# Clustered attention with a SoLU feed-forward layer on one core: the first batch's later head pairs loaded with both heads of a token side by side and sorted to clusters in one pass, u centred in place of w_out, and a new order by hand

## The chip, the cores and the metric

The kernel runs on one core of one Trainium2 chip. The metric is the device time of one execution in microseconds (us), the median of three runs. Both versions are compared by that number.

## The reference

Attention over B = 4 batches, H = 8 heads, S = 768 tokens, D = 64, in which a query sees only the keys of its own cluster, and then a feed-forward layer over all 3072 tokens. All inputs and the output are float32.

```python
q_n, k_n, c_n = (each row divided by its norm)            # centroids: [8, 16, 64]
q_assign = argmax(einsum('bhsd,hcd->bhsc', q_n, c_n), -1)  # 16 clusters a head
k_assign = argmax(einsum('bhsd,hcd->bhsc', k_n, c_n), -1)
mask = q_assign[:, :, :, None] == k_assign[:, :, None, :]
attn = softmax(where(mask, q @ k.T / sqrt(64), -1e9))
x = (attn @ v) with the heads side by side                 # [3072, 512]

h = x @ w_in                                               # [3072, 1024]
solu = h * softmax(h)
ln = (solu - mean(solu)) / sqrt(var(solu) + 1e-6) * g_ln
out = ln @ w_out                                           # [3072, 512]
```

## The kernel before, in words

**How it is built.** All work is cut into operations, each added with `add(name, engine, cost, key, function, needs, after, ...)` to an object of the class `Weave`. The order in which an engine runs them is written out by hand in five tables, `ORDER["SP"]`, `["POOL"]`, `["PE"]`, `["DVE"]`, `["ACT"]`: a kind of operation and a count, such as `E6` for the next six exponentials. `AWAY` lists the operations that another engine than their default one does. `run` only walks through these queues, so an engine does its operations strictly in the table's order and waits at each for what it needs.

**The attention.** 4 batches of 4 head pairs. For each pair q and k are loaded (`ld`, DMAs issued by SP), turned so that d lies on partitions (`tp` on PE at L396 and L403 with copies `xa`, `xb` out of PSUM at L422 and L430 for batch 0; `xt` on DVE for the others) into a tile xt, and cast to bf16 into qk (`ca`, L468 to L472). A product with the centroids (`cl`, on PE, PSUM tile csc) and four DVE steps (`tb`, `mx`, `oh`, `ot`) give a one-hot row of each token's cluster; 32 such rows are placed below the d rows of qk (`pl` on POOL, DVE or, as a DMA, on SP; `bl` blanks the other head's). With them the scores (`S`, L627, PE, into a ring of three PSUM banks sps or into a spare bank of hreg) come out so large where clusters agree that the exponential (`E`, L635, ACT) gives the mask too. `V` (L654, PE) multiplies e by v, which is loaded by `lv` and cast by `cv` (L558), and `N` (L666, L679, DVE) divides by the sum.

**E sets the shape of the start.** 294 E in all. Batch 0 has 24 of 384 columns for pair 0, whose tokens are done in two halves, and then 54 of 512 columns for pairs 1 to 3. So "the 25th E" is the first of pairs 1 to 3, and it needs pair 1's q and k, turned, cast and sorted to clusters.

**The loads of pairs 1 to 3 of batch 0.** `load_twelve` (L377) issues one DMA of 384 KB for q and one for k: a partition takes twelve tokens in a row, 3072 bytes, of head 0 on partitions 0 to 63 and of head 1 on 64 to 127. Once turned, even and odd tokens lie on the two halves of the partitions, not the two heads. So the copies sort by `by_two`, casts and placements write every other block (`every_other`), and the cluster product takes two accumulating passes (L484) with centroids masked by parity, `c_by_two`, which a second centroid transposition (`cq`, L909) and `cf` (L919) prepare in memory that w_out_c uses later.

**The feed-forward layer.** 24 tiles of 128 tokens, f = 0 to 23, six per batch, woven between the next batch's attention and, at the end, alone. For each: x turned (`tx`, a DMA), h = x @ w_in (`h`, L744, PE, into two of the three banks of hreg), its maximum (`hm`, L750, DVE), e = exp(h - max) with its sum (`ex`, L756, ACT), u = e * h (`u`, L763, DVE; three buffers), variance (`bn`, L774, and `ag`, L778, DVE), u turned into uT (`tu`: a DMA at L768, or for the last tiles `ptu` on PE, L732, with a copy at L738), y = uT @ w_out_c (`y`, L813, PE), a factor alpha per token (`at`, `al` on POOL), the evacuation times alpha (`sc`, L830 ACT or L832 DVE) and the store (`ou`, SP). The mean of solu is taken out beforehand, in the weights: w_out_c is g * w_out less its mean over d_ff. For that DVE sums g * w_out (`su`, L595 and L598, eight steps), PE takes the mean over partitions (`me`, L604, two matmuls) and DVE subtracts (`ce`, L607, eight steps).

**Around the start.** w_in and w_out are loaded by `li` and `lo`, four DMAs each; `wi` (L578, POOL) casts w_in to bf16. Until data comes PE runs idle matmuls (`wm`, 25 of them, and `fl`, two each, L859).

## Time and profile before

| | before |
|---|---|
| three runs, us | 224.49, 224.18, 224.29 |
| median, us | 224.29 |
| profiled execution: span from first to last instruction, us | 222.4 |
| profiled execution: instructions | 6852 |
| mean granted TensorE clock | 0.999 |
| DMA | 38.74 MB in 122,433 packets, 111,448 of them under 512 bytes |
| HBM | 23.11 MB read, 6.29 MB written |

The profile is of one execution, and its times count from the first instruction; the run time of an execution holds what lies around the span too, so the median stands 1.9 us above it. Engines: PE is the matrix engine, PEld its weight loads, DVE, ACT and POOL the vector, scalar and general engines, SP the one that only issues DMAs. A line of a group reads: source line, engine, operation, out<-in, the shapes, the count; then busy us and the mean ns of one; then the idle us just before these instructions and what ended most of it. A line of the timeline reads: start, length, engine, source line, operation, out<-in, count, and in brackets the wait before and who ended it. The windows view gives for each stretch its length, then busy us (and count) of PE, PEld, DVE, ACT and POOL, the granted clock, the share of the 16 DMA engines, and GB/s.

### The profile page before, as it was taken

Reading aid. Unit: us, or ns where it says so; the run is one execution under the profiler, and the core shown is the slowest. Engines: PE = TensorE matmul, PEld = TensorE weight load, DVE = VectorE, ACT = ScalarE, POOL = GpSimd, SP = SyncE. Lnnn points to the kernel's source line nnn. Section 1 sums busy time; section 2 is a strip of 40 time slices with the busy share of each in tenths; the row PEclk is TensorE's granted clock in tenths of the full one; section 3 lists DMA queues with packets and bytes.
Section 4 is the critical chain, followed back from the end, with each engine's and each line's share of the span. In section 5 each row is a group of like instructions: output and inputs, shape, how many; then the busy total and the mean of one; then the engine's idle time right before and its main releaser. Section 6 shows DMA issues by size and latency. Waiting matters only on the chain.

```text
span 222.4 us, 6852 instructions
## 1 busy us (share of the span) xinstructions
PE 214.8 (97%) x2518; PEld 151.8 (68%) x2548; DVE 199.1 (90%) x363; ACT 194.7 (88%) x382; POOL 126.6 (57%) x252
## 2 busy tenths in 40 slices
PE   8999899999999999999999999999999999999993
PEld 7765577767777687777777666676767767665452
DVE  2789999999999999899989999999999979999891
ACT  3899999999999999999999989999999989795352
POOL 3189597759884986188837674783746101226131
PEclk9999999999999999999999999999999999999999
DMA  6998989797799979899999897998922928565623
GB/s 157 352 388 221 193 165 284 203 172 165 127 175 237 180 141 215 136 193 166 153 211 239 156 185 150 151 168 158 230 99 50 115 78 145 117 165 121 166 98 143
DMA packets 122433, 38.74 MB, mean 174 GB/s; under 512 B 111448, under 2 KB 117152, under 8 KB 122400
## 3 DMA queue, kind: packets, MB, share of 16 engines
q1 hardware_dynamic: 121680, 37.82, 79.8%
q10 hardware_dynamic: 720, 0.49, 0.7%
q8 instruction: 20, 0.33, 0.7%
q14 instruction: 13, 0.11, 0.1%
HBM read 23.11 MB, written 6.29 MB: 132 GB/s over the span
## 4 chain that ended last, share of the span: by engine, by line
PE 91%; DVE 3%; issue 2%; ACT 2%; DVEq 0%; ACTq 0%
PE sps L627 27%; PE hreg L744 18%; PE yps L813 17%; PE ops L654 16%; PE csc L489 4%; PE hreg L627 2%; PE idle_p L859 2%; PE csc L484 1%; PE hreg L403 1%; PE hreg L396 1%; ACT qk L468 1%; PE hreg L813 1%; ACT e L635 1%; DVE u L763 1%; DVE w_sum L598 1%
## 5 line engine op out<-in xcount | busy, mean ns | idle before, releaser
L635 ACT ACTIVATE e<-sps 128x512 bf16<-128x512 f32 (+1 forms) x276 | 143.2, 609 | 10.2 <-PE sps L627 9.8
L627 PE MATMUL sps<-qk 96*128 96x256 bf16 (+5 forms) x600 | 87.4, 263 | 0.7 <-ACT e L635 0.4
L627 PEld LDWEIGHTS <-qk 96*128 96x128 bf16 (+1 forms) x636 | 59.6, 121 | 24.5 <-issue 8.8
L654 PEld LDWEIGHTS <-e 128*128 128x128 bf16 x1152 | 49.9, 97 | 9.3 <-issue 1.9
L654 PE MATMUL ops<-v,e 128*128 128x65 bf16 x1152 | 54.3, 193 | 0.4 <-DVE x L679 0.4
L744 PE MATMUL hreg<-w_in_sb,xT 128*128 128x512 bf16 x177 | 48.3, 378 | 0.8
L813 PE MATMUL yps<-w_out_c,uT 128*128 128x512 bf16 x169 | 45.1, 379 | 0.8
L540 POOL COPY qk<-oht 32x384 f32<-32x384 f32 (+1 forms) x49 | 24.2, 494 | 21.5 <-DVE oht L521 15.7
L763 DVE TENSOR_TENSOR u<-e_sb,hreg 128x1024 bf16<-128x1024 bf16 (+1 forms) x25 | 29.1, 1169 | 2.7 <-ACT e_sb L756 2.1
L774 DVE BATCH_NORM_STATS2 bs<-u 128x6 f32<-128x512 bf16 x48 | 31.3, 677 | 0.0
L750 DVE TENSOR_REDUCE nmax<-hreg 128x1 f32<-128x1024 f32 x24 | 29.1, 1213 | 2.0 <-PE hreg L744 1.7
L756 ACT ACTIVATE e_sb<-hreg,nmax 128x1024 bf16<-128x1024 f32 x24 | 26.9, 1121 | 4.5 <-DVE nmax L750 4.4
L790 POOL TENSOR_SCALAR esq<-es,mv 128x1 f32<-128x1 f32 x24 | 8.3, 344 | 33.6 <-DVE mv L778 30.3
L813 PEld LDWEIGHTS <-uT 128*128 128x128 bf16 x200 | 18.0, 97 | 13.1 <-issue 0.3
L744 PEld LDWEIGHTS <-xT 128*128 128x128 bf16 x192 | 17.6, 97 | 11.3 <-ACT e L635 0.3
L472 POOL TENSOR_SCALAR qk<-xt 64x768 bf16<-64x768 f32 (+1 forms) x27 | 22.2, 823 | 3.5 <-DVE xt L444 1.7
L444 DVE STREAM_TRANSPOSE xt<-raw 128x768 f32<-128x768 f32 x24 | 22.2, 949 | 0.0
L470 POOL CAST qk<-xt 64x768 bf16<-64x768 f32 (+1 forms) x25 | 20.9, 836 | 1.2
L679 DVE TENSOR_TENSOR x<-ops,den 128x256 bf16<-128x256 f32 (+1 forms) x39 | 18.9, 486 | 1.3
L784 POOL TENSOR_SCALAR es<-esum 128x1 f32<-128x1 f32 x24 | 5.6, 236 | 20.9 <-ACT e_sb L756 20.4
L793 POOL TENSOR_TENSOR alpha<-esq,halves 128x1 f32<-128x1 f32 x24 | 13.8, 574 | 2.0
L830 ACT ACTIVATE y<-yps,alpha 128x512 f32<-128x512 f32 x15 | 10.4, 695 | 4.3 <-PE yps L813 3.0
(85 smaller groups left out, 206.9 us busy)
## 6 DMA issues: line engine op xcount, KB each, us to landing
vf<-in_v_dram SPq DMA_DIRECT2D x16, 384.0 KB, 4.6
out_dram<-y SPq DMA_DIRECT2D x23, 256.0 KB, 2.5
raw<-in_q_dram SPq DMA_DIRECT2D x50, 96.0 KB, 3.8
raw<-in_k_dram SPq DMA_DIRECT2D x50, 96.0 KB, 3.0
w_g<-in_moe_w_out_dram SPq DMA_DIRECT2D x4, 512.0 KB, 8.3
w_st<-in_moe_w_in_dram SPq DMA_DIRECT2D x4, 512.0 KB, 6.2
raw<-in_q_dram SPq DMA_DIRECT2D x3, 384.0 KB, 6.0
raw<-in_k_dram SPq DMA_DIRECT2D x3, 384.0 KB, 7.8
```

Of the source, the lines that this page charges most:

```text
L444: nc.vector.transpose(xt[:], raws[b, p, i][:].rearrange("p j c -> p (j c)"))
L472: VEC[e].tensor_scalar(dst, src, scalar1=inv_C, scalar2=1.0, op0=Alu.mult, op1=Alu.mult)
L540: ins = VEC[e].tensor_copy(dst.bitcast(F32), src.bitcast(F32).unsqueeze(1) .to_broadcast([NB, 2, n // 2]))
L627: ins = nc.tensor.matmul(sps_[n, k][:, c0:c0 + w], side(b, h // 2, 1, h % 2, keys)[r], side(b, h // 2, 0, h % 2, slice(s0 * P, s0 * P + w) ...
L635: ins = nc.scalar.activation(es[n, k][:, :w], sps_[n, k][:, :w], Act.Exp, scale=exp_scale, bias=-exp_scale)
L654: nc.tensor.matmul(opss[g][:, s, :VW], es[n, k][:, c0:c0 + P], v1[slot(b, h // 2)][:, h % 2, kt, :VW], start=(kt == 0), stop=(kt == n_t - 1))
L744: uses(nc.tensor.matmul(hreg[:, at(f, f2)[1], :], xTs[f][:, dc, :], w_in_sb[:, dc, f2 * FF2:(f2 + 1) * FF2], start=(dc == 0), stop=(dc == ...
L750: uses(nc.vector.tensor_reduce(ff[f, "nmax"][:], pair_of(f), axis=AXY, op=Alu.max, negate=True), *both(f))
L756: uses(nc.scalar.activation(ff[f, "e"][:], pair_of(f), Act.Exp, bias=ff[f, "nmax"][:], accum_out=ff[f, "esum"][:]), *both(f))
L763: uses(nc.vector.tensor_tensor(ff[f, "u"][:, r], ff[f, "e"][:, r], pair_of(f)[:, r], op=Alu.mult), *both(f)[r])
L774: nc.vector.bn_stats(ff[f, "bs"][:, f2, :], ff[f, "u"][:, f2, :])
L813: ins = nc.tensor.matmul(dst, ff[f, "uT"][:, at(f, f2)[0] * (n_fc // 2) + c, :], w_out_c[:, fc, cols], start=(fc == fcs[0] and turn == 0 i ...
```

## The change

Four things are done together.

1. **Loads of pairs 1 to 3 of batch 0.** `load_pair` issues two DMAs of 192 KB for q and two for k, one a head. A partition takes six tokens in a row of a head, and the two heads of a token stand side by side in the tile: 768 pieces of 256 bytes a DMA. Turned, the two heads lie on the two halves of the partitions. `load_twelve`, `by_two`, `every_other`, `own_two`, `c_by_two`, `cq` and `cf` go; copies, casts and placements use the plain forms of the other batches, and the cluster product is one pass with `c_bd`.
2. **Centring.** w_out is only scaled by g (`scale_w_out`, `gw`, eight steps: five on POOL and three on DVE); `su`, `me` and `ce` go. u is made by an operation that also sums it over its row (su, over d_ff), and a new step `cu` replaces u in place by d_ff * u - su before the variance and the transposition: tiles 0, 1, 2, 5, 6, 10, 12, 14, 16, 19, 20, 22 on DVE, tile 23 in two halves on DVE, the other 11 on POOL. The small number in the root is scaled by d_ff.
3. **The first scores** have to come after all idle matmuls (`wm`, `fl`).
4. **New tables** `ORDER` and `AWAY`. Among much else, the copies and casts that ACT did among pair 0's E go to DVE and POOL or ahead of the first E, all four transpositions of pair 1 stand ahead of the first scores, the loads of w_out go behind those of w_in, ten instead of five placements are DMAs by SP, DVE has five fewer evacuations `sc`, and tile 22's copies of uT go from DVE to ACT.

The core of the diff, without what only falls away and without the costs in `add`, which now have no effect on the order:

```diff
...
     ORDER["PE"] = """
-        fl wm tp2 cp fl4 cl tp2 fl4 cl fl tp S2 cq S tp S tp S2 tp S tp2 S2 cl S V3 S2 tp3 S gt V3
+        fl7 wm tp2 cp tp fl cl fl tp fl tp2 cl tp2 S3 cl S3 tp2 S2 tp S tp S gt V3 S2 cl S V3 S2 tp
...
     ORDER["ACT"] = """
-        wa xa2 ca2 xa2 xb ca4 E6 xa E2 xa E xa ca E3 xa3 E4 ca E2 xa E53 ex E13 ex E5 sc E3 ex E11
+        wa xa xb xa ca2 xa ca xb xa2 ca xa E9 xa E64 ex E8 ex E12 ex sc E13 ex E4 sc E3 ex E3 sc E16
...
-    def load_twelve(b, p, i):
-        raws[b, p, i] = ld.tile([P, n_j, NB], F32, name="raw")
-        nc.sync.dma_start(out=raws[b, p, i][:].rearrange("p j c -> p (j c)"),
-                          in_=SRC[i][b, 2 * p:2 * p + 2].rearrange("h (q t) d -> (h q) (t d)",
-                                                                   q=D))
+    def by_turn(b, p, i):
+        return raws[b, p, i][:].rearrange("p j c -> p (j c)").rearrange("p (t m) -> p t m", m=P)
+
+    def load_pair(b, p, i, hh):
+        if (b, p, i) not in raws:
+            raws[b, p, i] = ld.tile([P, n_j, NB], F32, name="raw")
+        nc.sync.dma_start(out=by_turn(b, p, i)[:, :, hh * D:(hh + 1) * D],
+                          in_=SRC[i][b, 2 * p + hh].rearrange("(p t) d -> p t d", p=P))
...
-        if twelve(b, p):
-            dst = by_two(b, p, i).rearrange("p h t (q u) -> p h t u q", u=2)[:, :, :, hf, :]
-            src = src.rearrange("p (t h q) -> p h t q", h=2, q=D)
...
-        if twelve(b, p):
-            for c in range(4):
-                i, part = divmod(c, 2)
-                nc.tensor.matmul(csc[c * NB:(c + 1) * NB, :], c_by_two[:, p, 2 * part + hh, :],
-                                 by_two(b, p, i)[:, hh].rearrange("p t n -> p (t n)"),
-                                 start=(hh == 0), stop=(hh == 1), tile_position=(0, c * NB))
-        for c in range(4) if not twelve(b, p) else ():
+        for c in range(4):
...
-    def mean_w_out(x):
-        cols = slice(x * FF2 // 2, (x + 1) * FF2 // 2)
-        uses(nc.tensor.matmul(hreg[:, 2, cols], g_mean[:], w_sum[:, cols]), 2)
-
-    def centre_w_out(fc):
-        uses(nc.vector.scalar_tensor_tensor(out=w_out_c[:, fc, :], in0=w_g[:, fc, :],
-                                            scalar=g_ln2[:, fc:fc + 1], in1=hreg[:, 2, :],
-                                            op0=Alu.mult, op1=Alu.subtract), 2)
+    def scale_w_out(fc, e):
+        VEC[e].tensor_scalar(w_out_c[:, fc, :], w_g[:, fc, :], scalar1=g_ln2[:, fc:fc + 1],
+                             scalar2=None, op0=Alu.mult)
...
-        uses(nc.vector.tensor_tensor(ff[f, "u"][:, r], ff[f, "e"][:, r], pair_of(f)[:, r],
-                                     op=Alu.mult), *both(f)[r])
+        was = ff[f, "su"][:] if half else 0.0
+        ff[f, "su"] = sm.tile([P, 1], F32, name="su", bufs=6)
+        uses(nc.vector.tensor_tensor_reduce(
+            out=ff[f, "u"][:, r], in0=ff[f, "e"][:, r], in1=pair_of(f)[:, r], scale=1.0, scalar=was,
+            op0=Alu.mult, op1=Alu.add, accum_out=ff[f, "su"][:]), *both(f)[r])
+
+    def f_centre(f, e, half=None):
+
+        u = ff[f, "u"][:] if half is None else ff[f, "u"][:, half]
+        VEC[e].tensor_scalar(u, u, scalar1=float(d_ff), scalar2=ff[f, "su"][:], op0=Alu.mult,
+                             op1=Alu.subtract)
...
-        nc.gpsimd.tensor_scalar(ff[f, "es1"][:], ff[f, "esum"][:], scalar1=1e-3, scalar2=None,
+        nc.gpsimd.tensor_scalar(ff[f, "es1"][:], ff[f, "esum"][:], scalar1=1e-3 * d_ff, scalar2=None,
...
-        aft = ["S{}.{}".format(*BANKS[i - 1])] if i else []
+        aft = ["S{}.{}".format(*BANKS[i - 1])] if i else [nm for nm in wv.by if re.match("wm|fl", nm)]
...
```

What the tables do is seen in the instructions as they stand. On PE, at the first scores, before (idle_p is the product of the idle matmuls, hreg<-ident_f,raw a transposition `tp`, sps the scores `S`, cps the second centroid transposition `cq`):

```order
L859 LDWEIGHTS w_out_c
L859 MATMUL idle_p<-w_out_c 128x128
L403 MATMUL hreg<-ident_f,raw 128x128 x3
L627 LDWEIGHTS qk_99
L627 MATMUL sps<-qk_99 128x384
L627 LDWEIGHTS qk_99
L627 MATMUL sps<-qk_99 128x384
L909 MATMUL cps<-ident_f,c_n 128x128
```

And now (csc is the cluster product `cl` of pair 0's second half; each x6 is two transpositions `tp` of pair 1):

```order
L825 LDWEIGHTS w_out_c
L825 MATMUL idle_p<-w_out_c 128x128
L400 MATMUL hreg<-ident_f,raw 128x128 x6
L467 MATMUL csc<-xt,c_bd 32x192 x4
L400 MATMUL hreg<-ident_f,raw 128x128 x6
L584 LDWEIGHTS qk_99
L584 MATMUL sps<-qk_99 128x384
```

Before, one of pair 1's four transpositions stood ahead of the first scores and the others among them; now all four, the two of q and the two of k, stand ahead of them.

On ACT, at pair 0's exponentials, before (e<-sps are the E; xt<-hreg copies `xa` out of PSUM; qk<-xt casts `ca`; qk_99 belongs to pair 0, qk_101 to pair 2):

```order
L468 ACTIVATE qk_99<-xt 64x384 x4
L635 ACTIVATE e<-sps 128x384 x6
L430 COPY xt<-hreg 128x384
L635 ACTIVATE e<-sps 128x384 x2
L430 COPY xt<-hreg 128x384
L635 ACTIVATE e<-sps 128x384
L430 COPY xt<-hreg 128x384
L468 ACTIVATE qk_101<-xt 64x6x128
L635 ACTIVATE e<-sps 128x384 x3
L430 COPY xt<-hreg 128x384 x3
L635 ACTIVATE e<-sps 128x384 x4
L468 ACTIVATE qk_101<-xt 64x6x128
```

And now (qk_100 belongs to pair 1):

```order
L454 ACTIVATE qk_99<-xt 64x384
L419 COPY xt<-ops 128x3x64
L424 COPY xt<-hreg 128x384 x2
L454 ACTIVATE qk_100<-xt 64x768
L424 COPY xt<-hreg 128x384
L592 ACTIVATE e<-sps 128x384 x9
L424 COPY xt<-hreg 128x384
L592 ACTIVATE e<-sps 128x384 x15
L592 ACTIVATE e<-hreg 128x512 x2
```

Of the seven copies and two casts among pair 0's 24 E, one copy is left there; a cast and copies of pair 1 stand ahead of the first E instead.

On DVE, at the last tiles, before (nmax<-hreg is `hm`, uT<-utp a copy of the turned u, bs and mv the variance, w_in_sb<-hreg,alpha an evacuation `sc`):

```order
L750 TENSOR_REDUCE nmax<-hreg 128x1
L738 COPY uT<-utp 128x512 x2
L774 BN_STATS bs<-u 128x6
L778 BN_AGGR mv<-bs 128x2 x2
L763 TENSOR_TENSOR u<-e_sb,hreg 128x512 x2
L774 BN_STATS bs<-u 128x6 x2
L778 BN_AGGR mv<-bs 128x2
L738 COPY uT<-utp 128x512
L832 TENSOR_SCALAR w_in_sb<-hreg,alpha 128x192
```

And now (L722 is u with its sum, two instructions each time; L729 the centring `cu`):

```order
L707 TENSOR_REDUCE nmax<-hreg 128x1
L740 BN_STATS bs<-u 128x6 x2
L722 ISA u,su<-e_sb,hreg 128x512
L722 ISA su 128x1
L744 BN_AGGR mv<-bs 128x2
L722 ISA u,su<-e_sb,hreg,su 128x512
L722 ISA su 128x1
L729 TENSOR_SCALAR u<-u,su 128x512
L744 BN_AGGR mv<-bs 128x2
L729 TENSOR_SCALAR u<-u,su 128x512
L740 BN_STATS bs<-u 128x6
L695 COPY uT<-utp 128x512
```

The last u's two halves and both centrings now stand ahead of its variance and of the copy of uT; the transposition on PE, which lies between, reads the centred u, where before it read u as it was made.

More of the change, by code (lines that the diff above doesn't have):

```diff
@@ L924 @@
     add("cb", "DVE", 0.27, -500, lambda e: keep_centroids(), ["cp"], give="m")
-    add("cq", "PE", 0.28, 0, lambda e: turn_centroids(), ["cn"], ["cp"], take="m")
-    add("cf", "DVE", 0.65, -490, lambda e: keep_by_two(), ["cq"], give="m")
     def before(idx, back):
@@ L1206 @@
             for half in range(2):
-                add(made[half], "DVE", 0.6, s + half, (lambda e, f=f, half=half: f_u(f, half)),
+                add(made[half], "DVE", 0.66, s + half, (lambda e, f=f, half=half: f_u(f, half)),
                     nd + made[:half])
+            flat = [f"cu{f}.{half}" for half in range(2)]
+            for half in range(2):
+                add(flat[half], "DVE", 0.22, s + 2 + half,
+                    (lambda e, f=f, half=half: f_centre(f, e, half)), made)
         else:
             made = [f"u{f}"] * 2
-            add(f"u{f}", "DVE", 1.22, s, (lambda e, f=f: f_u(f)), nd)
+            add(f"u{f}", "DVE", 1.25, s, (lambda e, f=f: f_u(f)), nd)
+            flat = [f"cu{f}"] * 2
+            add(f"cu{f}", "POOL", 1.1, s + 1, (lambda e, f=f: f_centre(f, e)), made[:1],
+                also={"DVE": 0.36})
+        made = flat
         kept = [f"y{f - 3}.3"] if f >= 3 else []
```

212 lines of the change are left out of this document (82 added, 130 removed).

## The prediction

> **What bounds the kernel now.** I read the page's engine totals first, then the busy time by stage, then the chain of waits. The page:
>
> ```profile
> PE 214.8 (97%) x2518; PEld 151.8 (68%) x2548; DVE 199.1 (90%) x363; ACT 194.7 (88%) x382; POOL 126.6 (57%) x252
> PE 91%; DVE 3%; issue 2%; ACT 2%; DVEq 0%; ACTq 0%
> ```
>
> The second line is the chain that ended last: PE for 91% of the span. That is an average; the windows view by stage (stretch, length, busy us of PE, PEld, DVE, ACT, POOL, clock, DMA share, GB/s) shows two regimes:
>
> ```profile
> 10.00:24.00 14.00, 13.18 (x145) 8.50 (x144) 12.71 (x26) 13.60 (x34) 10.93 (x18) 1.00 0.96 315
> 24.00:50.00 26.00, 25.38 (x349) 18.66 (x351) 24.83 (x48) 25.48 (x53) 18.84 (x34) 1.00 0.92 196
> 50.00:205.00 155.00, 153.33 (x1781) 110.00 (x1809) 145.56 (x252) 144.28 (x277) 89.78 (x171) 1.00 0.82 158
> 205.00:222.00 17.00, 13.93 (x83) 7.20 (x82) 11.40 (x20) 6.05 (x10) 4.11 (x11) 1.00 0.46 140
> ```
>
> Up to 50 us the first batch's exponentials (E) run on ACT without a hole (13.60 of 14, 25.48 of 26); DMA and DVE are nearly full too. From 50 to 205 us PE is full (153.3 of 155) while ACT has 10.7 us and DVE 9.4 us free. So an edit counts through the moment at which the first batch's E are done, and a PE saving before 50 us counts only as far as ACT gets there sooner. I work with five terms: A, when the first E starts; B, its 24 E of pair 0; C, the 54 E of pairs 1 to 3; D, 50 to 205 us; E, the end. The median 224.29 is 1.9 us above the profiled span of 222.4; I take the sum against the span and keep the 1.9.
>
> **Edits that leave PE cheaper.** From the chain in order of time, one cluster product in two passes, in one pass, and half of the mean of w_out:
>
> ```profile
> 13.68 1.43 PE csc L484 x16
> 34.45 0.78 PE csc L489 x8
> 37.78 0.43 PE hreg L604 x2
> ```
>
> Three products save 3 × 0.65 = 1.95 us, the mean 0.86, the second centroid transposition about 0.2: 3.0 us of PE, all before 42 us, where ACT sets the pace. I book none of it by itself; it would count if ACT had holes there.
>
> **Term A, the first E.** Two things push it out. The order puts 14 warm-up matmuls ahead of the block of 25 where there were 2. The timeline:
>
> ```profile
> 0.97 3.06 PE L859 MATMUL idle_p<-w_out_c 128*128 128x128 bf16 x27 [0.97 <-DVE halves L863]
> 3.96 1.01 PE L396 MATMUL hreg<-ident_f,raw 64*64 64x64 f32 x25
> 4.95 0.94 ACT L422 COPY xt<-hreg 128x384 f32<-128x384 f32 x2 [0.84 <-PE hreg L396]
> ```
>
> 27 took 3.06, so 39 take 4.4, and the first transposition starts at about 5.3 instead of 3.96, ACT's first copy at 6.3 instead of 4.95. And all four transpositions of pair 1 now stand ahead of the first scores, so the first E waits for pair 1's k. Issues and landings (KB, us to landing) of pair 1's q and k:
>
> ```profile
> 3.33 0.43 SPq L377 DMA_DIRECT2D raw<-in_q_dram  x1
> 3.80 0.43 SPq L377 DMA_DIRECT2D raw<-in_k_dram  x1
> ...
> raw<-in_q_dram SPq DMA_DIRECT2D x1, 384.0 KB, 5.0
> ...
> raw<-in_k_dram SPq DMA_DIRECT2D x1, 384.0 KB, 5.5
> ```
>
> They land at 8.33 and 9.30, 0.97 apart: that is one transfer of 384 KB, and the first could begin to count at 7.36. Now each becomes two of 192 KB in 768 pieces of 256 bytes. The DMA view of a stretch with 128-byte packets alone (32.5 to 35 us) and of one with long packets (9 to 11 us):
>
> ```profile
> DMA packets 3074, 0.39 MB, mean 154 GB/s; under 512 B 3074, under 2 KB 3074, under 8 KB 3074
> q1 hardware_dynamic: 3074, 0.39, 96.1%
> ...
> DMA packets 429, 0.81 MB, mean 406 GB/s; under 512 B 40, under 2 KB 284, under 8 KB 429
> q1 hardware_dynamic: 429, 0.81, 105.5%
> ```
>
> That is 2.5 × 16 × 0.961 / 3074 = 12.5 ns for 128 bytes and 2 × 16 × 1.055 / 429 = 79 ns for 1.9 KB; the line between them gives 17.3 ns for 256 bytes, 768 / 16 × 17.3 = 0.83 us a load. The ends are 192 KB at 406 GB/s, 0.48, and at 154 GB/s, 1.28; I take 0.83, since it lies close to the 128-byte row. Pair 1's fourth load lands at 7.36 + 4 × 0.83 = 10.7 (9.3 to 12.5). Two transpositions and ACT's copy behind it, about 1.5, give a first E at 12.2; ACT's own list, 13 steps from 6.3, gives at least 11.5. The first E was at 10.61: **A = +1.6** (+0.9 to +3.3).
>
> The Trainium skill, "DMA: Bandwidth & Descriptors", section "Why small descriptors are slow (HBM only)", charges a 256-byte descriptor 11 cycles where 8 carry data; by that a load would take about 0.62 us (an estimate), A would be near +0.9 and the sum 0.7 lower. No run here shows 256-byte loads from DRAM; the 128-byte row is already dearer than such a rule, so the sum keeps 0.83.
>
> **Term B, ACT among pair 0's 24 E.** ACT's timeline:
>
> ```profile
> 10.61 2.34 ACT L635 ACTIVATE e<-sps 128x384 bf16<-128x384 f32 x6
> ...
> 15.33 0.84 ACT L468 ACTIVATE qk<-xt 64x768 bf16<-64x768 f32 x1
> 16.08 1.22 ACT L635 ACTIVATE e<-sps 128x384 bf16<-128x384 f32 x3
> 17.19 1.27 ACT L430 COPY xt<-hreg 128x384 f32<-128x384 f32 x3
> 18.34 1.63 ACT L635 ACTIVATE e<-sps 128x384 bf16<-128x384 f32 x4
> ...
> 24.56 0.60 ACT L635 ACTIVATE e<-hreg 128x512 bf16<-128x512 f32 x1
> ```
>
> Between the first and the 25th E it now also makes seven copies (0.38 each from start to start, 17.19 to 18.34) and two casts (0.75, 15.33 to 16.08). The new order leaves one copy: 6 × 0.4 + 2 × 0.75 = 4.0 us go. They go to DVE and POOL or ahead of the first E. New waits take some back: v of pair 0 stands behind eight short-piece loads, landing at 7.36 + 8 × 0.83 + 1 = 15.0 where its product ran at about 15; DVE has four more copies ahead of pair 1's first scores. I take 0.9 (0.3 to 3). **B = -3.1**, and the 25th E comes at 23.1 instead of 24.56.
>
> **Term C, 24 to 50 us.** ACT's list is the same. DVE loses the sum and the centring of w_out and gains little:
>
> ```profile
> L598 DVE SCALAR_TENSOR_TENSOR w_sum<-w_g,g_ln,w_sum 128x512 f32<-128x512 f32 x7 | 5.9, 837 | 0.1
> L607 DVE SCALAR_TENSOR_TENSOR w_out_c<-w_g,g_ln,hreg 128x512 bf16<-128x512 f32 x8 | 5.5, 740 | 0.0
> L558 DVE CAST v<-vf 128x384 bf16<-128x384 f32 x7 | 2.4, 357 | 0.0
> L578 POOL CAST w_in_sb<-w_st 128x512 bf16<-128x512 f32 x8 | 4.7, 614 | 2.5 <-DMA w_st<-in_moe_w_in_dram 2.4
> L763 DVE TENSOR_TENSOR u<-e_sb,hreg 128x1024 bf16<-128x1024 bf16 (+1 forms) x25 | 29.1, 1169 | 2.7 <-ACT e_sb L756 2.1
> L887 DVE CUSTOM_DVE_ANT_0 c_n<-c_all 128x64 f32<-128x64 f32 x1 | 0.2, 226 | 1.5 <-DMA c_all<-in_centroids_dram 1.5
> L887 DVE DVE_READ_ACCUMULATOR2_ANT c_nsq<- 128x1 f32 x1 | 0.1, 83 | 0.0
> ```
>
> Out: 5.9 + 0.8 + 5.5 = 12.2 us. In: three scalings on DVE at about 0.4 (the cast's rate, 357 ns for 384), five on POOL at 0.61. The load order moves w_out behind w_in, so w_in, on which the first h waits, is not later; w_out lands a few us before its first product. ACT stays the bound; DVE's slack may spare it the odd wait: **C = -0.5** (-1 to +1).
>
> **Term D, 50 to 205 us.** PE's work is unchanged, so D is 0 unless u comes late. Each u now sums itself: the row of such a fused form has 226 ns for 64 elements plus 83 for the read. At one element a cycle (u's own 1024 in about 1.2 us) that is +0.1 a tile, 24 × 0.1 = 2.4 us. Centring adds 12 × 0.4 = 4.8 on DVE (from the cast's rate; between 0.36 and u's 1.2) and 11 × 1.2 on POOL, which has 65 us free. Five evacuations leave DVE, 3.7 us. DVE's net of 3.5 stands against 9.4 free. The later centred u delays the transposition and y by 0.4 to 1.5 us, and PE's order has 8 to 20 us of other work between a tile's h and its y. **D = 0** (-0.5 to +1.5).
>
> **Term E, the end.** The last tile:
>
> ```profile
> 213.88 1.24 DVE L763 TENSOR_TENSOR u<-e_sb,hreg 128x512 bf16<-128x512 bf16 x2
> 214.94 0.39 PE L732 MATMUL utp<-ident_b,u 128*128 128x128 bf16 x4
> 217.11 1.91 PE L813 MATMUL hreg<-w_out_c,uT 128*128 128x320 bf16 x16
> ```
>
> PE turned the first half of u while the second was made. Now both halves and two centrings (0.3 each) come first: about 1.3 later, of which y of tile 22 hides most, as it did from 215 to 217. **E = +0.5** (0 to +1).
>
> Sum: 1.6 - 3.1 - 0.5 + 0 + 0.5 = -1.5: a span of 220.9 and a time of **222.8 us**.
>
> **The rivals.**
> 1. *The short pieces set the pace (slower).* Place: the DMA engines from 6 to 24 us, at 0.96 busy already. At the 128-byte rate a load takes 1.28: pair 1 lands at 12.5 (A = +3.3), v of pair 0 at 18.6, pair 3 near 24; the 25th E comes near 26.3 instead of 24.56. With C and E: 224.29 + 1.75 - 0.5 + 0.5 = 226.0. It decides from about 1.1 us a load on. For it: that DMA share. Against: the line gives 0.83. The Trainium skill, "DMA: Bandwidth & Descriptors", "Specifications", wants 512 bytes for line rate and names a read-modify-write below; the 154 GB/s row agrees that short is slow.
> 2. *ACT's relief is eaten.* What ACT sheds DVE must do before the same scores, and DVE was 12.71 of 14 busy: B only -1.6, so 224.3, no change.
> 3. *Larger gain.* If the short loads are quick (A +0.9), B loses nothing to waits (-4.0) and C gives -1: 224.29 - 0.9 + 0.9 - 4.0 - 1.0 + 0.5 = 219.8.
> 4. *DVE becomes the bound after 50 us.* If the fused u needs two cycles an element, 24 × 1.1 = 26 us come on top of 9.4 free: 224.3 + 17, about 240. The 226 ns speak against it: 64 elements at two cycles leave 93 ns for what costs the other small vector operations over 150.
>
> **How the numbers follow.** A measurement tells 0.2%, 0.45 us, from no change. Forecast (faster by 0.5 to 3.5): 0.49; rival 3: 0.11; rival 2: 0.15; rival 1: 0.17; rival 4 or a late centred u: 0.08. Faster 0.60, same 0.15, slower 0.25. The range 219.8 to 226.0 reaches from rival 3 to rival 1 and leaves out rival 4 and the far ends. The forecast's own range is 220.8 to 223.8.
>
> **What would show it.** Right: the first E near 12.2, the 25th near 23, PE as full as now after 50 us, the last output matmul 1.5 us earlier than 217.11 + 1.91. A wrong: a first E before 11 or after 13.5. B wrong: ACT waiting for PE more than 1 us in all before the 25th E. D wrong: a fused u above 1.4 us, or PE waiting for uT. The forecast falls if the 25th E is no earlier than 24.5.

## The result, and the profile after

The changed kernel takes 250.28 us (median of four runs, 249.77 to 251.29) where the kernel before takes 224.24: a ratio of 1.117, with a 95% interval of 1.1141 to 1.1199. The forecast was 222.8, faster. The profiled execution has a span of 247.8 us; its page gives these totals and the chain that ended last:

```profile
PE 221.5 (89%) x2519; PEld 152.2 (61%) x2519; DVE 199.0 (80%) x387; ACT 196.6 (79%) x382; POOL 174.6 (70%) x258
PE 46%; POOL 22%; DVE 14%; DMA 7%; issue 5%; ACT 3%; SPq 2%; POOLq 0%; DVEq 0%; ACTq 0%
```

PE's share of the chain has gone from 91% to 46%, and POOL, which had no share, holds 22%. By stage (the windows view, columns as before):

```profile
10.00:24.00 14.00, 12.75 (x139) 8.86 (x140) 12.19 (x29) 11.77 (x28) 10.25 (x19) 1.00 0.97 215
24.00:50.00 26.00, 23.20 (x321) 16.31 (x319) 22.37 (x47) 25.31 (x52) 19.59 (x31) 1.00 0.95 239
50.00:205.00 155.00, 139.07 (x1550) 97.35 (x1551) 124.63 (x224) 127.81 (x244) 118.77 (x162) 0.97 0.74 146
205.00:248.00 43.00, 37.95 (x352) 22.91 (x350) 34.85 (x70) 26.40 (x50) 22.49 (x32) 0.98 0.48 121
```

From 50 to 205 us no engine is full: PE 139 of 155 where it had 153, DVE 125, ACT 128, POOL 119. No single engine's work fills this stage, so its length has to come from what the engines wait for. POOL's busy time there rose from 89.8 to 118.8. The groups that are new (busy, mean ns of one, idle before):

```profile
L729 POOL TENSOR_SCALAR u<-u,su 128x1024 bf16<-128x1024 bf16 x11 | 40.9, 3718 | 9.5 <-DVE su L722 7.7 <-DVE den L623 1.0
L722 DVE CUSTOM_DVE_ANT_0 u<-e_sb,hreg 128x1024 bf16<-128x1024 bf16 (+1 forms) x24 | 28.6, 1191 | 6.9 <-ACT e_sb L713 6.3
L565 POOL TENSOR_SCALAR w_out_c<-w_g,g_ln 128x512 bf16<-128x512 f32 x5 | 8.1, 1626 | 0.1
L729 DVE TENSOR_SCALAR u<-u,su 128x1024 bf16<-128x1024 bf16 (+1 forms) x14 | 6.8, 486 | 0.2
```

A centring takes 0.49 us on DVE and 3.72 us on POOL; a scaling of w_out takes 1.63 us on POOL. The u with its sum costs what u cost before (1.19 us against 1.17), and 0.08 us more for reading the sum. How one such instruction holds others up is seen in the timeline (start, length, engine, what ran, and in brackets the wait before it):

```profile
77.66 3.71 POOL L729 TENSOR_SCALAR u<-u,su 128x1024 bf16<-128x1024 bf16 x1 [1.09 <-DVE su L722]
81.45 0.23 POOL L750 TENSOR_SCALAR es<-esum 128x1 f32<-128x1 f32 x1
81.75 0.50 POOL L513 COPY qk<-oht 32x384 f32<-32x384 f32 x1
82.30 0.38 PE L584 MATMUL sps<-qk 80*128 80x256 bf16 x2 [0.91 <-POOL qk L513]
82.77 1.25 ACT L592 ACTIVATE e<-sps 128x512 bf16<-128x512 f32 x2 [0.51 <-PE sps L584]
...
85.03 0.57 POOL L759 TENSOR_TENSOR alpha<-esq,halves 128x1 f32<-128x1 f32 x1
85.63 0.69 ACT L796 ACTIVATE y<-yps,alpha 128x512 f32<-128x512 f32 x1 [1.61 <-POOL alpha L759]
85.71 3.71 POOL L729 TENSOR_SCALAR u<-u,su 128x1024 bf16<-128x1024 bf16 x1
```

The placement at 81.75 stood behind the centring that began at 77.66. The scores at 82.30 waited for that placement and the E at 82.77 for those scores, and the evacuation at 85.63 waited for an alpha that stood further back in the same queue. Three scalings of w_out do the same at 54 us, with 3.3 us in which PE stands before a score:

```profile
54.00 4.96 POOL L565 TENSOR_SCALAR w_out_c<-w_g,g_ln 128x512 bf16<-128x512 f32 x3
...
61.06 0.41 POOL L522 MEMSET qk<- 16x384 f32 x1
...
61.53 0.64 PE L584 MATMUL sps<-qk 96*128 96x256 bf16 x4 [3.33 <-POOL qk L522]
```

Such a stand of PE costs more than its length. Three times the trace grants PE half its clock for 3.41 us, from 62.20, 144.12 and 195.32 us on. Each time PE had gone on 0.5 to 0.7 us earlier, after it had stood for 1.9 to 3.3 us. A row of the windows view, and h's two matmuls inside and outside such a stretch:

```profile
62.20:65.61 3.41, 3.41 (x23) 2.18 (x22) 1.09 (x1) 2.13 (x4) 1.54 (x4) 0.50 0.83 147
145.97 1.06 PE L701 MATMUL hreg<-w_in_sb,xT 128*128 128x512 bf16 x2
148.21 0.59 PE L701 MATMUL hreg<-w_in_sb,xT 128*128 128x512 bf16 x2
```

The three stretches cost up to 3 × 3.41 / 2 = 5.1 us of PE's work, an estimate. In the kernel before, the clock is halved only behind the last matmul. The length of the stand doesn't decide alone: one of 3.04 us, up to 176.47 us, had no such stretch behind it.

The start is another matter. A table of three moments, each counted as an E in the trace of a profiled execution, and of the span, in us. The 79th E is the first of batch 1; versions of the experiments below stand with them.

| kernel | first E | 25th E | 79th E | span | from the 79th E to the end |
|---|---|---|---|---|---|
| before | 10.61 | 24.56 | 52.84 | 222.4 | 169.6 |
| changed | 12.35 | 23.56 | 52.68 | 247.8 | 195.1 |
| changed, centring and scaling on DVE | 12.13 | 23.34 | 52.94 | 233.4 | 180.5 |
| changed, POOL subtracts a tensor | 11.53 | 23.44 | 52.75 | 230.0 | 177.3 |
| changed, no centring | 11.69 | 23.15 | 52.01 | 225.7 | 173.7 |
| the same, long pieces | 11.09 | 22.59 | 50.97 | 227.2 | 176.2 |
| before, u centred on DVE | 10.67 | 24.08 | 54.79 | 232.5 | 177.7 |
| before, no centring | 10.57 | 24.00 | 52.73 | 222.3 | 169.6 |
| before, loads by head in short pieces | 9.82 | 27.08 | 55.55 | 225.0 | 169.4 |
| before, loads by head in long pieces | 9.59 | 25.60 | 53.88 | 223.3 | 169.4 |

Some executions took over 1.5% longer than the fastest of the same version; below, "Measured" is the median of all, the ratios leave those out and are the numbers to compare, and the third row's profile is of one of them (236.9 us against a median of 233.2). The changed kernel, then, is even with the old one when batch 1 begins, and all of the loss comes after that: 25.5 us. PE stood idle for 20.8 us in that part where it had stood 5.0, and it was busy for 9.7 us more (174.3 us where it had 164.6), part of which is the halved clock.

### The profile page after: what moved, and what is told of

It is laid out like the page before. It is cut to its first block, busy times and chain, and to the rows that moved or that the text cites. A ratio compares the mean times of both kernels' runs of the same rounds, so it can differ in the third digit from the quotient of the medians.

```text
span 247.8 us, 6881 instructions
## 1 busy us (share of the span) xinstructions
PE 221.5 (89%) x2519; PEld 152.2 (61%) x2519; DVE 199.0 (80%) x387; ACT 196.6 (79%) x382; POOL 174.6 (70%) x258
## 4 chain that ended last, share of the span: by engine, by line
PE 46%; POOL 22%; DVE 14%; DMA 7%; issue 5%; ACT 3%; SPq 2%; POOLq 0%; DVEq 0%; ACTq 0%
PE sps L584 14%; PE hreg L701 12%; PE yps L779 9%; PE ops L611 8%; POOL u L729 5%; POOL qk L513 4%; PE csc L467 3%; DVE u L722 2%; POOL qk L458 2%; DMA w_g<-in_moe_w_out_dram 2%; DMA raw<-in_k_dram 2%; POOL v L531 2%; POOL w_out_c L565 2%; ACT e L592 2%; DVE bs L740 2%
## 5 line engine op out<-in xcount | busy, mean ns | idle before, releaser
L584 PE MATMUL sps<-qk 96*128 96x256 bf16 (+5 forms) x600 | 97.1, 268 | 12.2 <-POOL qk L522 7.1
L611 PEld LDWEIGHTS <-e 128*128 128x128 bf16 x1152 | 55.4, 99 | 18.0 <-issue 4.0
L611 PE MATMUL ops<-v,e 128*128 128x65 bf16 x1152 | 61.7, 195 | 3.5 <-DVE x L636 3.4
L701 PE MATMUL hreg<-w_in_sb,xT 128*128 128x512 bf16 x192 | 56.2, 393 | 1.2 <-DVE su L722 1.1
L779 PE MATMUL yps<-w_out_c,uT 128*128 128x512 bf16 x184 | 50.9, 379 | 0.0
L729 POOL TENSOR_SCALAR u<-u,su 128x1024 bf16<-128x1024 bf16 x11 | 40.9, 3718 | 9.5 <-DVE su L722 7.7
L722 DVE CUSTOM_DVE_ANT_0 u<-e_sb,hreg 128x1024 bf16<-128x1024 bf16 (+1 forms) x24 | 28.6, 1191 | 6.9 <-ACT e_sb L713 6.3
L458 POOL TENSOR_SCALAR qk<-xt 64x768 bf16<-64x768 f32 (+1 forms) x29 | 25.0, 863 | 1.6
L796 ACT ACTIVATE y<-yps,alpha 128x512 f32<-128x512 f32 x21 | 14.6, 695 | 11.4 <-POOL alpha L759 9.1
L531 POOL CAST v<-vf 128x384 bf16<-128x384 f32 x27 | 14.3, 531 | 5.5 <-PE sps L584 4.6
```

What stands on the lines that cost most here:

```text
L458: VEC[e].tensor_scalar(dst, src, scalar1=inv_C, scalar2=1.0, op0=Alu.mult, op1=Alu.mult)
L584: ins = nc.tensor.matmul(sps_[n, k][:, c0:c0 + w], side(b, h // 2, 1, h % 2, keys)[r], side(b, h // 2, 0, h % 2, slice(s0 * P, s0 * P + w) ...
L611: nc.tensor.matmul(opss[g][:, s, :VW], es[n, k][:, c0:c0 + P], v1[slot(b, h // 2)][:, h % 2, kt, :VW], start=(kt == 0), stop=(kt == n_t - 1))
L701: uses(nc.tensor.matmul(hreg[:, at(f, f2)[1], :], xTs[f][:, dc, :], w_in_sb[:, dc, f2 * FF2:(f2 + 1) * FF2], start=(dc == 0), stop=(dc == ...
L722: uses(nc.vector.tensor_tensor_reduce(out=ff[f, "u"][:, r], in0=ff[f, "e"][:, r], in1=pair_of(f)[:, r], scale=1.0, scalar=was, op0=Alu.mul ...
L729: VEC[e].tensor_scalar(u, u, scalar1=float(d_ff), scalar2=ff[f, "su"][:], op0=Alu.mult, op1=Alu.subtract)
```

## The experiments

The first theory (P): the price of POOL's instruction. Its rivals: the new order itself (O), the longer chain from u to its transposition (U), DVE's work (V), SP's order of loads (S). Every ratio below is to the kernel before on the same chip, with its 95% interval.

**All centrings on DVE.** In the order, each of POOL's eleven goes right behind its u on DVE:

```diff
-  POOL: ... cv pl cu at pl cv pl ca al cu cv ...
+  POOL: ... cv pl at pl cv pl ca al cv ...
-  DVE:  ... bn oh ot ag u N xt hm ...
+  DVE:  ... bn oh ot ag u cu N xt hm ...
```

> The changed kernel with all centrings of u on DVE, each right behind its u; the scaling of w_out stays where it was. Theory P (the price of one instruction on POOL): a centring on POOL took 3.72 us where 1.2 was forecast, 11 of them 40.9 us, and the casts, placements and blanks queued behind it hold the scores up. Then POOL's busy time falls by 40.9 us, DVE's rises by 11 x 0.49 = 5.4, and the time comes to about 228 us: 224 and the 4 us lost to the scaling of w_out on POOL at 54 to 61 us. Rival O (the new order itself feeds the exponentials too late) and rival U (centring u in place delays its transposition wherever it is done) both keep it above 243 us.

Measured: 235.97 us, 1.0509 (1.0458 to 1.0559). More than half of the loss went, as P has it, but 8 us less than P expected.

**All scalings of w_out on DVE.** The five `gw` of POOL's order go to where DVE has its three.

> The changed kernel with all eight scalings of w_out on DVE; the centrings stay where they were. Theory P: five scalings at 1.63 us (8.1 us) leave POOL, the hole of 3.3 us in the scores at 58 to 61.5 us goes, and the time falls by 3 to 4 us to 246 to 247. Rivals O and U: no change, 250 us.

Measured: 245.73 us, 1.0966 (1.092 to 1.1012): 4.6 us less, as P has it. They took 1.63 us on POOL and 0.59 on DVE, and the casts behind them came sooner.

**Both.**

> Both of the foregoing: POOL does neither centring nor scaling. Theory P: the 79th exponential (the first of batch 1) at 52.5 us as now, no hole behind it over 1 us, and 222.8 to 226 us in all; above 224.3 if DVE, which gets 7.5 us more work, is what then waits. Rivals O and U: above 240 us.

Measured: 233.22 us, 1.0423 (1.0396 to 1.0449). The 79th E came at 52.94, as expected, but the time stayed 7 us above P's range: P explains 17 of the 26 us, and something else the rest.

**A constant in place of the sum.** In POOL's centring alone, which leaves the subtraction out:

```diff
-        VEC[e].tensor_scalar(u, u, scalar1=float(d_ff), scalar2=ff[f, "su"][:], ...)
+        nc.gpsimd.tensor_scalar(u, u, scalar1=float(d_ff), scalar2=0.0, ...)
```

> The changed kernel in its own order, with the second operand of the centring on POOL a constant 0 in place of the sum per partition: it leaves out the subtraction in those 11 tiles. It parts two causes of the price of 3.72 us. If the operand per partition makes it, an instruction takes 1.2 to 1.8 us (the cast with two constants took 0.88 for 64 x 768), and theory P gives 250.3 - 11 x 2.2 = 226 to 231 us, the order and the chain of steps being the same. If the size or the type makes it, it stays at 3.7 us and the time at 250. Rivals O and U give 245 or more even if the instruction is short.

Measured: 248.33 us, 1.1068 (1.101 to 1.1126). Each of the eleven still took 3.69 us, so the operand per partition is not what makes the instruction slow.

**Forms of POOL's instruction by themselves.** Seven of them behind the kernel before, twice over:

```diff
+    for _ in range(2):
+        nc.gpsimd.tensor_scalar(fb, fa, scalar1=1024.0, scalar2=0.0, op0=Alu.mult, op1=Alu.subtract)
+        nc.gpsimd.tensor_scalar(fb, fa, scalar1=1024.0, scalar2=fs, op0=Alu.mult, op1=Alu.subtract)
+        nc.gpsimd.tensor_scalar(fb, fa, scalar1=fs, scalar2=None, op0=Alu.mult)
+        ... (64 partitions; 512 columns)
+        nc.gpsimd.tensor_tensor(fb, fa, fs.to_broadcast([P, 1024]), op=Alu.subtract)
+        nc.gpsimd.tensor_copy(fb, fa)
```

> The kernel before, with seven forms of POOL instruction behind each other at its end, twice, on 1024 bf16 columns: two constants; a constant and an operand per partition (the centring); an operand per partition alone (the scaling's form); the centring on 64 partitions; the centring on 512 columns; a subtraction of the operand as a tensor; a plain copy. With two constants the centring stayed at 3.69 us in the run before this one, so the operand does not make the price. If arithmetic on 128 partitions does, the form on 64 partitions takes about 1.2 us (the cast with two constants took 0.87 for 64 x 768), the copy about 1.4 (0.53 for 128 x 384), and the others 3 to 3.7. If bf16 input does, all but the scaling's share 3.7, the one on 64 partitions too.

The timeline of POOL at the end of that run:

```profile
217.42 3.65 POOL L1297 TENSOR_SCALAR qk<-w_out_c 128x1024 bf16<-128x1024 bf16 x1
221.17 3.71 POOL L1298 TENSOR_SCALAR qk<-w_out_c,g_ln 128x1024 bf16<-128x1024 bf16 x1
224.98 2.84 POOL L1299 TENSOR_SCALAR qk<-w_out_c,g_ln 128x1024 bf16<-128x1024 bf16 x1
227.92 3.70 POOL L1300 TENSOR_SCALAR qk<-w_out_c,g_ln 64x1024 bf16<-64x1024 bf16 x1
231.73 2.00 POOL L1301 TENSOR_SCALAR qk<-w_out_c,g_ln 128x512 bf16<-128x512 bf16 x1
233.81 1.89 POOL L1302 TENSOR_TENSOR qk<-w_out_c,g_ln 128x1024 bf16<-128x1024 bf16 x1
235.77 1.04 POOL L1303 COPY qk<-w_out_c 128x1024 bf16<-128x1024 bf16 x1
```

The second round gave the same within 0.02 us. The price goes by columns (2.00 for 512, 3.71 for 1024), not by partitions (3.70 for 64 of them) nor by the operand, and the form decides: two operations on one tensor 3.65 to 3.71, one operation 2.84, two tensors 1.89, a copy 1.04. The Trainium skill, "GPSIMD Engine Reference", section "Engine selection", has it otherwise: about twice VectorE's time where there are two inputs, near line rate with one. Here the form with one tensor in took twice as long as that with two.

**POOL's other form.** On the version with the scaling on DVE (245.7 us), the same eleven centrings in the same places of POOL's queue, by the mean and a subtraction:

```diff
+            m = sm.tile([P, 1], F32, name="m", bufs=2)
+            nc.gpsimd.tensor_scalar(m[:], ff[f, "su"][:], scalar1=1.0 / d_ff, scalar2=None, op0=Alu.mult)
+            nc.gpsimd.tensor_tensor(flat, flat, m[:].to_broadcast([P, d_ff]), op=Alu.subtract)
```

> The changed kernel in its own order, scaling on DVE (245.7 us), the 11 centrings on POOL in another form: the mean by one small instruction and a subtraction as a tensor, 1.89 us for 1024 columns where the form with operands per partition took 3.71, together about 2.2. POOL loses 17 us. Theory P (the price of the instruction): 234 to 239 us, and more than 3 us above 233 if the queue behind it still holds casts and placements up. Rivals that put the loss elsewhere: 244 us or more.

The two groups in its profile:

```profile
L731 POOL TENSOR_TENSOR u<-u,m 128x1024 bf16<-128x1024 bf16 x11 | 20.8, 1893 | 0.9
L728 POOL TENSOR_SCALAR m<-su 128x1 f32<-128x1 f32 x11 | 2.4, 222 | 7.8 <-DVE su L719 6.5 <-DVE den L620 1.0
```

Measured: 232.25 us, 1.0383 (1.0358 to 1.0408). POOL lost 17.7 us of work, the kernel 13.5 us of time, with every other operation in its place. That is the sharpest test of P, and it holds; the time is 2 us below P's range, and as low as with the centrings on DVE. Part of the gain came by way of the clock: its mean was 0.976 to 0.992 in the executions of the version with the scaling on DVE, and 0.996 to 1.0 here.

**More loads ahead (S).** On the version with both on DVE, as many loads of batches 1 to 3 ahead of each transposition on SP as in the kernel before.

> Centring and scaling on DVE (233.2 us), and on SP as many loads of batches 1 to 3 ahead of each transposition of x and u as in the kernel before. Theory S (SP's order): the loads of batch 1's third pair were issued at 53.4 us where the kernel before has them at 42.2, since they stand behind the transposition of the first u, which waits for its centring; and loads go on late through batch 2. Then the matrix engine's holes from 50 to 205 us shrink and the time falls to 225 to 229 us. Rival V (DVE, which has the centrings now, is what waits): 232 to 234 us, no change.

Measured: 234.29 us, 1.0457 (1.0426 to 1.0487), no gain. The first loads of batch 1's third pair were issued at 45.0 us, where the version with both on DVE had them at 53.4 and the kernel before at 42.2. They did come sooner and it brought nothing, so S falls.

**No centring, in the new order.** The step's instruction is left out; the rest as with both on DVE:

```diff
     def f_centre(f, e, half=None):
         u = ...
-        VEC[e].tensor_scalar(u, u, scalar1=float(d_ff), scalar2=ff[f, "su"][:], op0=Alu.mult,
-                             op1=Alu.subtract)
+        return
```

> The changed kernel with scaling on DVE and no centring at all: it leaves the mean of u out of the computation, everything else in the same order as the version with both on DVE (233.2 us). Theory C (what is left of the loss is the centring, as work on DVE or as a step in the chain): DVE has 13.9 us less, and the time is 222.5 to 225 us. Rival O (the new order or the short loads cost it): 229 us or more.

Measured: 229.0 us, 1.022 (1.0166 to 1.0273). Both sides had a part: by the ratios 4.5 us go with the centring, and 5 us remain without it.

**Less DVE work, same chain.** On the version with both on DVE, the variance from the first half of u alone:

```diff
-        nc.vector.bn_stats(ff[f, "bs"][:, f2, :], ff[f, "u"][:, f2, :])
+        if f2 == 0:
+            nc.vector.bn_stats(ff[f, "bs"][:, f2, :], ff[f, "u"][:, f2, :])
```

> Both on DVE (233.2 us), without the second half of each tile's variance: it leaves 24 statistics of 0.68 us, 16 us of DVE's work, out, and keeps every step from u over its centring to the transposition. It parts two causes of the 9 us left: theory V, DVE's work: 224 to 227 us. Theory U, the chain of steps of each tile: 231 us or more.

Measured: 231.48 us, 1.0351 (1.0292 to 1.041). DVE's busy time fell by over 14 us, the time by 1.7: in the new order DVE's work is not what counts, and V falls there. To leave out the centring, 12 us of DVE's busy time, brought 4.5, which points to its place between u and the transposition more than to its work, as U has it.

**Long pieces, in the new order.** The version without centring, its loads in pieces of 3072 bytes:

```diff
-        nc.sync.dma_start(out=by_turn(b, p, i)[:, :, hh * D:(hh + 1) * D],
-                          in_=SRC[i][b, 2 * p + hh].rearrange("(p t) d -> p t d", p=P))
+        nc.sync.dma_start(out=raws[b, p, i][hh * D:(hh + 1) * D].rearrange("p j c -> p (j c)"),
+                          in_=SRC[i][b, 2 * p + hh].rearrange("(q t) d -> q (t d)", q=D))
```

> The version without centring (229.0 us), with the twelve loads of pairs 1 to 3 in pieces of 3072 bytes instead of 256, one head on each half of the partitions: tokens and heads come out in another arrangement, so it leaves the right sorting out, while every instruction, its engine and its place stay. If the short pieces make the 5 us that stand above the kernel before: 224 to 226 us, with the first exponential about 1 us earlier. If the new order makes them: 228 to 229.5 us.

Measured: 229.56 us, 1.0265 (1.0208 to 1.0321): no gain. The table shows more: the 79th E came 1 us sooner, and the end did not. In this order a sooner start is lost again later. The 79th E comes before that of the kernel before with either length of piece, so the 5 us are lost behind these loads: they are the order's. Six loads in place of twelve were not tried in this order.

**The parts alone, in the old order.** First the loads by head and the product in one pass:

> The kernel before in its own order with the first part of the change alone: the loads of 192 KB by head and the cluster product in one pass, w_out centred as before. The second head of pair 1's k landed near 10.6 us in the changed kernel, 9.30 before, and v of pair 0 four loads later; against that stand 1.95 us less on the matrix engine and 0.65 on DVE. The theory that the short pieces cost nothing that counts: 223.5 to 225 us. The rival that they set the pace of the start: 225.5 to 227 us.

Measured: 226.87 us, 1.0142 (1.0102 to 1.0181). The first E was earlier (9.82), but the 25th came at 27.08 and the 79th at 55.55, 2.7 us late; from there on it ran as the kernel before. The rival holds by its number. The trace shows by which way: w_out's loads stand behind these in SP's queue, and DVE waited 1.55 us, up to 21.94, for the first of them before it summed w_out. What stands behind that in DVE's queue came late, and PE stood 2.0 us, up to 24.53, for the division of pair 0's result. The changed kernel has no such sum. To part the pieces from their number, each load of 384 KB was only cut in two, in long pieces:

```diff
-        nc.sync.dma_start(out=raws[b, p, i][:].rearrange("p j c -> p (j c)"),
-                          in_=SRC[i][b, 2 * p:2 * p + 2].rearrange("h (q t) d -> (h q) (t d)", q=D))
+        nc.sync.dma_start(out=raws[b, p, i][hh * D:(hh + 1) * D].rearrange("p j c -> p (j c)"),
+                          in_=SRC[i][b, 2 * p + hh].rearrange("(q t) d -> q (t d)", q=D))
```

> The kernel before with each load of 384 KB of pairs 1 to 3 cut into two of 192 KB, one a head, in its own long pieces of 3072 bytes; the rest as before, two passes included. The kernel before with the short pieces took 226.9 us against 224.0. If the pieces made that: 224 to 224.6 us here. If twelve issues and landings in place of six made it: 226 to 227.5.

Measured: 225.29 us, 1.0076 (1.0048 to 1.0105). That lies between the two expectations: about half of the loss comes from twelve loads in place of six, the other half from the pieces (with the one pass). DVE waited for w_out here too, 1.35 us.

Then u centred, everything of it on DVE, in the old order:

> The kernel before in its own order with the second part of the change alone: u with its sum and centred, each centring right behind its u, w_out only scaled, all on DVE. Rival V: DVE gets 24 x 0.49 + 24 x 0.1 = 14 us more between 50 us and the end, where it had 9.4 us free, so 227 to 230 us. Theory S: the cost is nearly hidden, 224 to 226 us.

Measured: 233.14 us, 1.0411 (1.0337 to 1.0485). And the same without the centring's instruction:

> The kernel before in its own order with w_out scaled on DVE, u with its sum, and no centring: it leaves the mean out. With centring on DVE in this order it took 233.1 us. If the centring's 14.6 us of DVE made that: 223.5 to 225.5 us, and then the version without centring in the new order (229.0) shows 4 to 5 us that the loads and the new order cost by themselves. If the scaling on DVE at 44 to 52 us made part of it: 226 to 228 us.

Measured: 224.15 us, 1.0025 (0.9997 to 1.0053), no change against the kernel before. The windows view of 50 to 205 us, first with the centring on DVE:

```profile
50.00:205.00 155.00, 150.05 (x1714) 105.51 (x1738) 149.92 (x279) 140.25 (x269) 87.27 (x161) 1.00 0.77 149
```

and without it:

```profile
50.00:205.00 155.00, 154.97 (x1810) 110.06 (x1810) 145.81 (x274) 144.16 (x276) 89.84 (x171) 1.00 0.82 156
```

In the old order the version with the 14.6 us of centring on DVE is 9 us slower, and DVE (the third engine in the row) is at 149.9 of 155 then, with PE down by 5. Between 50 and 215 us DVE waited for others only 1.7 us in all: it has become the limit. V holds there in kind, but the time is 3 us above its range. Of the 9 us, 2 stand already at the 79th E, ahead of which there is one centring: three scalings of w_out took 4.4 us there and 2.2 in the other profile, and why was not tried. What the last row shows beside it: leaving away the sum, the mean and the centring of w_out, 0.9 us of PE and, less the scaling's 6.2, 6 us of DVE before 50 us, brings nothing.

**A longer chain, in the old order.** u plain, its mean from the variance's statistics, and 22 subtractions on POOL of 1.9 us each:

```diff
+            nc.gpsimd.tensor_tensor(u, u, ff[f, "mv"][:, 0:1].to_broadcast([P, d_ff]), op=Alu.subtract)
```

> The kernel before in its own order and with its own loads, w_out scaled alone (on DVE), u plain, its mean taken from the variance's statistics, which follow u at once, and taken off u by POOL's subtraction as a tensor (1.89 us) for 22 tiles and by DVE for the last two. DVE has no more work than before behind 50 us, but a tile's transposition comes about 4 us later behind its u. Theory U (the longer chain from u to the transposition costs by itself): 228 us or more. Theory V (only work on a full DVE or a queue on POOL costs): 223 to 226 us.

Measured: 249.16 us, 1.1051 (1.0999 to 1.1104). The group, and a piece of the chain that ended last (start, length, what):

```profile
L752 POOL TENSOR_TENSOR u<-u,mv 128x1024 bf16<-128x1024 bf16 x22 | 42.3, 1922 | 18.1 <-DVE mv L770 16.4 <-DVE den L649 0.7 <-POOL qk L548 0.5
```

```profile
73.51 1.23 DVE u L746
74.76 1.30 DVE bs L766 x2
76.22 0.53 DVE oht L520
76.87 0.51 POOL qk L539
77.45 1.90 POOL u L752
79.41 0.50 POOL qk L539
79.97 0.50 POOL qk L539
80.52 0.50 POOL qk L539
```

And its row of the windows view:

```profile
50.00:205.00 155.00, 142.80 (x1592) 98.55 (x1589) 132.36 (x225) 130.08 (x248) 116.45 (x171) 0.98 0.75 140
```

POOL had about the same work as in the changed kernel (116.5 us against 118.8), in a cheap form, with DVE at 132 of 155, and the loss was nearly the same. PE had half its clock for 3.41 us twice here, again around the end of stands of 2.5 and 2.6 us. So it is not the length of one instruction alone: a centring that POOL's queue must wait for (16.4 us of waiting) and then carry holds back the placements behind it, as the chain shows. This run lengthens the chain and loads POOL's queue at once; it does not part the two.

## Why the prediction was wrong

The step that failed is term D, and in it the words "11 × 1.2 on POOL, which has 65 us free" and "**D = 0** (-0.5 to +1.5)". From the 79th E to the end the kernel went from 169.6 to 195.1 us; the forecast had no change but +0.5 at the end.

- *The price.* The prediction names no row for the 1.2 us. DVE's u (1.17 us) gives it, and so does POOL's cast of w_in (614 ns for 512 columns). The kernel before even had the same operation on POOL, k's cast:

```profile
L472 POOL TENSOR_SCALAR qk<-xt 64x768 bf16<-64x768 f32 (+1 forms) x27 | 22.2, 823 | 3.5 <-DVE xt L444 1.7
```

  That gives 1.1 us for 1024 columns. But it reads float32 with two constants and multiplies twice; no row of POOL's read bf16. The fault is that 1.2 stood as certain, with no bound upwards: 3.72 was measured. The scalings (0.61 forecast, 1.63 measured) failed by the same step. Moving or cheapening these took the ratio from 1.117 to 1.0383: some 17 to 18 of the 26 us.
- *The free time.* Idle time of a queue that works in order is not room for a step of any length. In the same places of POOL's queue, eleven steps of 2.1 us cost no more than the centrings on DVE (1.0383 against 1.0423), and eleven of 3.7 us cost 13 us more. In the kernel before, the largest part of POOL's 65 us of idle time from 50 to 205 us was this wait (us in all, times, the longest):

```profile
POOL esq L790 <- DVE mv L778: 29.6, 13, 5.1
```

  POOL stood there for DVE, and yet PE waited for POOL nowhere in that stage. A centring put among casts and placements makes these late, and the scores behind them.
- *The cover.* "PE's order has 8 to 20 us of other work between a tile's h and its y" did not cover it, since what came late was not y but the next scores. So the signs that it named for a wrong D did not show: the fused u took 1.19 us and PE did not wait for uT, but 8.9 us for blanks and placements by POOL. With POOL's price out of the way, on DVE alone, the centring still cost 9 us in the old order (DVE at 149.9 of 155) and 4.5 us in the new one.
- *The order.* No rival held a loss from the new order by itself. Without any centring it stands at 1.022, the old one at 1.0025; neither more loads ahead nor long pieces nor less DVE work brought it back. Its chain shows DVE's queue at 50 to 55 us and a late transposition at 78 us, but no run took these away: which waits make the 5 us stays open.
- *The clock.* No term held that PE's clock could change, and up to 5 us of the loss are its three halved stretches.
- *Terms A and B* held. The first E came at 12.35 (12.2 forecast), by one of its two causes alone: the warm-up matmuls pushed ACT's first copy to 5.40 and not to 6.3 (39 took 3.86 us, not 4.4), and the wait for pair 1's k decided. ACT then ran with little of what it had between:

```profile
11.97 0.48 ACT L424 COPY xt<-hreg 128x384 f32<-128x384 f32 x1 [1.17 <-PE hreg L400]
12.35 3.80 ACT L592 ACTIVATE e<-sps 128x384 bf16<-128x384 f32 x9
16.02 0.50 ACT L424 COPY xt<-hreg 128x384 f32<-128x384 f32 x1
17.01 1.25 ACT L592 ACTIVATE e<-sps 128x384 bf16<-128x384 f32 x3 [0.49 <-PE ops L611]
18.49 0.49 ACT L592 ACTIVATE e<-sps 128x384 bf16<-128x384 f32 x1 [0.22 <-PE sps L584]
19.29 4.40 ACT L592 ACTIVATE e<-sps 128x384 bf16<-128x384 f32 x11 [0.31 <-PE sps L584]
23.56 1.11 ACT L592 ACTIVATE e<-hreg 128x512 bf16<-128x512 f32 x2
```

  The 24 E took 11.21 us in place of 13.95, a gain of 2.7 where 3.1 was forecast (its 4.0 of copies and casts adds up to 3.9), with the waits of 1.0 in brackets; "more than 1 us" was its sign of being wrong, and it sits on that edge. Pair 1's k landed at 10.95 (the chain's row, first of the next two fences; 10.7 forecast), and between 5.5 and 6.7 us, with 256-byte pieces alone, the DMA view gives 1.2 × 16 × 1.078 / 1163 = 17.8 ns a piece (17.3 forecast), 0.85 us a load:

```profile
5.47 5.48 DMA raw<-in_k_dram
```

```profile
q1 hardware_dynamic: 1163, 0.29, 107.8%
```

  By the rule of the Trainium skill, "DMA: Bandwidth & Descriptors", section "Why small descriptors are slow (HBM only)", a load would have taken about 0.62 us, as the prediction estimated; the measurement decides against it.
- *Term C* was -0.5 and measured +0.84 (29.12 us from the 25th to the 79th E, 28.28 before), inside its bounds. With it the gain at the start was gone: 0.16 us at the 79th E.
- *Term E* held: from the start of the last u's first half to the end 9.0 us in place of 8.5, with these rows between:

```profile
238.81 0.69 DVE L722 CUSTOM_DVE_ANT_0 u<-e_sb,hreg 128x512 bf16<-128x512 bf16 x1
...
240.72 0.30 DVE L729 TENSOR_SCALAR u<-u,su 128x512 bf16<-128x512 bf16 x1
...
242.18 1.91 PE L779 MATMUL hreg<-w_out_c,uT 128*128 128x320 bf16 x16
```

- *The rivals.* Rival 4 asked for a slow u on DVE; u took 1.19 us, and the rival was of the right stage and sign, but of the wrong engine. "A late centred u" stands only in the line of chances, without a price. Rival 3's sum takes off 0.9 that none of its terms gives: they add up to 220.7, not 219.8. Rival 1's loads did cost 1.4% in the old order, and nothing that can be told in the new one.

No version here beats the kernel before, and none of the parts alone does: the best of them, without any centring in the old order, is level with it, and it leaves the mean out.

## What to carry to other kernels

Price an operation that moves to another engine by a row of that engine in that form, input type and operations included (the same instruction on other input gave 1.1 us where 3.7 came). Where no row has the form, treat its price as unknown, with a wide bound upwards; one run with the forms behind each other settles it. The idle time of an engine that works strictly in order is not simply room: ask what stands behind the new instruction in its queue, and who waits for that. And when every engine has slack and the time is longer, look at the hand-overs between the queues: 14 us less work on DVE brought 1.7 us, while 18 us less of the one instruction that stood ahead of POOL's placements brought 13.

## What the runs showed of the hardware

POOL's elementwise forms lie far apart on the same 1024 columns: 1.04 us for a copy, 1.89 for two tensors, 2.84 and 3.7 for one tensor with one and two scalar operations, the last the same on 64 as on 128 partitions. One row does not fit: the cast of k, two multiplications by constants on float32 in, took 0.88 us for 768 columns in the changed kernel. Neither constants alone (3.65 us on bf16) nor float32 alone (the scaling, 1.63 us for 512 columns) makes a form quick; which combination does was not tried.

PE's granted clock fell to half for 3.41 us at a time, around or shortly after the end of stands of 1.9 to 3.3 us, three times in the changed kernel and twice in the last experiment's; h's two matmuls then took 1.06 us in place of 0.59.
